# Plain products with whole rows of weights in the first batch's second layer, and its weight sums made a batch later

## The chip, the cores and the metric

The kernel runs on one core of a Trainium2 chip. The metric is the device time of one execution in microseconds (us). Each version was run several times, always beside the kernel before on the same chip; medians are quoted. A profile is one execution out of these, and its "span" is about 1.8 us shorter than the time of the same execution.

Engines in the profile: PE is TensorE (PEld its weight loads), DVE is VectorE, ACT is ScalarE, POOL is GpSimd, SP issues the DMAs. `L1085` is a line of the kernel; L550 is the helper through which all of VectorE's two-input operations go, so these are told apart by their tiles (`s<-h`, `w<-w`).

## The reference

Four batches of 768 x 512. After an attention, each batch goes through a Fourier mix, a normalisation and a channel MLP in float32:

```python
# x: the attention's output, (4, 768, 512)
X = np.fft.fft(np.fft.fft(x, axis=1), axis=2)
u = x + np.real(X).astype(np.float32)
mu = np.mean(u, axis=-1, keepdims=True)
var = np.mean((u - mu) ** 2, axis=-1, keepdims=True)
un = (u - mu) / np.sqrt(var + 1e-06)
ch = np.maximum(un @ w_ch1, 0.0) @ w_ch2      # (512, 2048), then (2048, 512)
return (u + ch).astype(np.float32)
```

The weights come as float64.

## The kernel before

Both layers of the MLP ("h" and "o") multiply in 2x2 blocks with seven block products in place of eight, at the price of sums of blocks: left sums of the first operand, right sums of the second. A batch's MLP goes in two chunks of four hidden tiles (NC = 4): h of chunk 0, o of chunk 0, h of chunk 1, o of chunk 1. In the first batch the weights are converted from float64 piece by piece on VectorE and ScalarE, while the products run; the finished tiles, four blocks and sums in seven slots, are stored to scratch memory, and the later batches only load them.

```python
def _right_sums(tt, b):
    tt(b(T1), b(B12), b(B11), ALU.subtract)
    tt(b(T2), b(B22), b(T1), ALU.subtract)
    tt(b(T3), b(B22), b(B12), ALU.subtract)
    tt(b(T4), b(B21), b(T2), ALU.subtract)
...
    def tt(out, in0, in1, op):                      # L550, VectorE
        nc.vector.tensor_tensor(out=out, in0=in0, in1=in1, op=op)
    def gtt(out, in0, in1, op):                     # L553, GpSimd
        nc.gpsimd.tensor_tensor(out=out, in0=in0, in1=in1, op=op)
...
    def block_sums(b, gg):                          # for the attention of batch b
        ...
        if b == 1:
            tt(raw[0], raw[0], raw[1], ADD)
            nc.vector.tensor_reduce(out=vb, in_=raw[0].rearrange("p f d -> p d f"), op=ADD, axis=AX.X)
        else:
            gtt(raw[0], raw[0], raw[1], ADD)
            while hf > 2:
                hf //= 2
                gtt(raw[0][:, 0:hf], raw[0][:, 0:hf], raw[0][:, hf:2 * hf], ADD)
            gtt(vb, raw[0][:, 0], raw[0][:, 1], ADD)
...
    def make(f, j):                                 # first batch: weight tile j of layer f
        ...
        for hh in range(2):
            yield from convert((f, j, hh), wv[:, 2 * hh:2 * hh + 2].rearrange("p a n -> p (a n)"))
        (_left_sums if f == 1 else _right_sums)(tt, lambda i: wv[:, i])
        yield
        stores.append((to, wv))
        ...
    def get_w2(b, j):
        w = bpool.tile([P, 7, HD], FP, tag="w2", bufs=NC, name=f"w2_{b}_{j}")
        if b == 0:
            return
        fetch(out=w, in_=dw2[j])
        wt[2, b, j] = w
...
    def gen_channel(b):
        ...                                         # h of the chunk, L1038
            for i in range(HT):                     # o: three pairs of row tiles
                ...
                tt(left[S1], a21, left[A22], ADD)   # left sums s<-h
                tt(left[S2_], left[S1], left[A11], SUB)
                tt(left[S3], left[A11], a21, SUB)
                tt(left[S4], left[A12], left[S2_], SUB)
                ...
                def product(ps, a, r, start, stop): # L1085
                    for n, j in enumerate(js):
                        nc.tensor.matmul(ps, left[a][:, n, :], wt[2, b, j][:, r, :], start=start and n == 0,
                                         stop=stop and n == NC - 1, skip_group_check=True)
                product(X, A11, B11, True, False)
                tt(x11, X, x11, ADD)
                ...                                 # six more products, each with its addition
```

Of the kernel before, what the change touches and what calls it, by code (L numbers as in the profile page):

```python
# [16 lines left out]
P = 128  # L17
# [447 lines left out]
def _left_sums(tt, a):  # L465
    tt(a(S1), a(A21), a(A22), ALU.add)
    tt(a(S3), a(A11), a(A21), ALU.subtract)
    tt(a(S2_), a(S1), a(A11), ALU.subtract)
    tt(a(S4), a(A12), a(S2_), ALU.subtract)
# [9 lines that stand above are left out]
def _main_program(ctx, tc, q, k, v, moe_w_ch1, moe_w_ch2, out):  # L479


    nc = tc.nc
    B, H, S, D = q.shape
    DM = H * D
    DF = moe_w_ch1.shape[1]
    NST = S // P
# [11 lines left out]
    NJ = NIT // 2  # L498
    NC = 4
    D1 = D + 1  # L500
    assert (S, DM, D, H % 4, NDT, NJ % NC, WK) == (768, 512, 64, 0, 4, 0, 96)
    ADD, SUB = ALU.add, ALU.subtract
# [30 lines left out]
    dw2 = [dpool.tile([P, 7, HD], FP, name=f"dw2_{j}") for j in range(NJ)]  # L533
# [3 lines left out]
    def fetch(out, in_):  # L537

        ins = nc.sync.dma_start(out=out, in_=in_)
        if in_order[0]:  # L540
            tc.keep_in_program_order(ins)
# [4 lines left out]
    def bank(shape, name):  # L546
        return psum.tile(shape, FP, tag="bank", bufs=4, name=name)

    def tt(out, in0, in1, op):
        nc.vector.tensor_tensor(out=out, in0=in0, in1=in1, op=op)  # L550
# [248 lines left out]
    wt, issued = {}, set()  # L799
# [45 lines left out]
    def make(f, j):  # L845


        if f == 1:
            w = bpool.tile([P, 7, 2, P], FP, tag="w1", bufs=3, name=f"w1_0_{j}")
            wv, to = w.rearrange("p a k n -> p a (k n)"), dw1[j].rearrange("p a k n -> p a (k n)")  # L850
        else:
            w = wv = bpool.tile([P, 7, HD], FP, tag="w2", bufs=NC, name=f"w2_0_{j}")
            to = dw2[j]
        for hh in range(2):
            yield from convert((f, j, hh), wv[:, 2 * hh:2 * hh + 2].rearrange("p a n -> p (a n)"))
        (_left_sums if f == 1 else _right_sums)(tt, lambda i: wv[:, i])
        yield
        stores.append((to, wv))
        if len(stores) > 2 or len(pieces) == len(raws):
            fetch(out=stores[0][0], in_=stores.pop(0)[1])  # L860
        wt[f, 0, j] = w
        yield

    def gen_weights():
        for f, j, stage in plan:
            while stage and stage not in issued:
                yield
            steps = make(f, j)
            while True:

                with tc.issue_after(marks[stage]) if stage in marks else ExitStack():
                    done = next(steps, steps) is steps
                if done:
                    break
                yield
        for to, wv in stores:
            fetch(out=to, in_=wv)

    def get_w1(b, j):
        w = bpool.tile([P, 7, 2, P], FP, tag="w1", bufs=3, name=f"w1_{b}_{j}")  # L880
        if b == 0:
            return
        fetch(out=w, in_=dw1[j])
        wt[1, b, j] = w

    def get_w2(b, j):
        w = bpool.tile([P, 7, HD], FP, tag="w2", bufs=NC, name=f"w2_{b}_{j}")
        if b == 0:
            return
        fetch(out=w, in_=dw2[j])  # L890
        wt[2, b, j] = w


    tables = {}
# [127 lines left out]
    def gen_channel(b):  # L1022
        x, u = x_of[b], wt["u", b]
        for c in range(NJ // NC):
            js = range(NC * c, NC * (c + 1))
            h = bpool.tile([P, NC, 2, S], FP, tag="h", name=f"h_{b}_{c}")
            for j in js:
                if 0 < j < NJ - 2:
                    get_w1(b, j + 2)
                get_w2(b, j)  # L1030
                w = wt[1, b, j]
                c11, c12 = h[:, j - NC * c, 0, 0:S2], h[:, j - NC * c, 0, S2:S]
                c21, c22 = h[:, j - NC * c, 1, 0:S2], h[:, j - NC * c, 1, S2:S]
                X, Y, Z = (bank([P, S2], f"h{n}_{b}_{j}") for n in "xyz")

                def product(ps, a, r, start, stop):
                    for kk in range(2):
                        nc.tensor.matmul(ps, w[:, a, kk, :], u[:, r, kk, :], start=start and kk == 0,  # L1038
                                         stop=stop and kk == 1, skip_group_check=True)

                def relu(t):
                    if b:
                        nc.vector.tensor_scalar(out=t, in0=t, scalar1=0.0, scalar2=None, op0=ALU.max)
                    else:
                        nc.scalar.activation(out=t, in_=t, func=AF.Relu)

                product(X, A11, B11, True, False)
                nc.scalar.copy(out=c11, in_=X)  # L1048
                product(Y, A12, B21, True, True)
                tt(c11, Y, c11, ADD)  # L1050
                yield
                product(X, S2_, T2, False, False)
                nc.scalar.copy(out=c12, in_=X)
                product(Z, S1, T1, True, False)
                nc.scalar.copy(out=c22, in_=Z)
                relu(c11)
                yield
                product(X, S3, T3, False, False)
                tt(c22, X, c22, ADD)
                product(Z, S4, B22, False, True)  # L1060
                tt(c12, Z, c12, ADD)
                yield
                product(X, A22, T4, False, True)
                nc.scalar.activation(out=c21, in_=X, func=AF.Relu)  # L1064
                relu(c22)
                relu(c12)
                issued.add(("h", b, j))
                yield
            for i in range(HT):
                t1, t2 = slice(P * i, P * (i + 1)), slice(S2 + P * i, S2 + P * (i + 1))  # L1070
                left = {A11: h[:, :, 0, t1], A12: h[:, :, 1, t1], A22: h[:, :, 1, t2]}
                for s in (S1, S2_, S3, S4):
                    left[s] = bpool.tile([P, NC, P], FP, tag="s", bufs=5, name=f"s{s}_{b}_{c}_{i}")
                a21 = h[:, :, 0, t2]
                tt(left[S1], a21, left[A22], ADD)
# [3 lines that stand above are left out]
                X, Y, Z = (bank([P, HD], f"o{n}_{b}_{c}_{i}") for n in "xyz")  # L1079
                x11, x12 = x[:, i, 0:HD], x[:, i, HD:DM]  # L1080
                x21, x22 = x[:, HT + i, 0:HD], x[:, HT + i, HD:DM]
# [8 lines that stand above are left out]
                product(Y, A12, B21, True, True)  # L1090
                tt(x11, Y, x11, ADD)
                yield
                product(X, S2_, T2, False, False)
                tt(x12, X, x12, ADD)
                product(Z, S1, T1, True, False)
                tt(x22, Z, x22, ADD)
                yield
                product(X, S3, T3, False, False)
                tt(x22, X, x22, ADD)
                product(Z, S4, B22, False, True)  # L1100
                tt(x12, Z, x12, ADD)
                yield
                product(X, A22, T4, False, True)
                tt(x21, X, x21, ADD)
                if NC * (c + 1) == NJ:
                    for t in (i, HT + i):
                        fetch(out=out[b, P * t:P * (t + 1), :], in_=x[:, t, :])
                if i == HT - 1:
                    issued.add(("o", b, c))
                yield  # L1110

    def gen_post(b):
        yield from gen_fourier(b)
        yield from gen_channel(b)
# [52 lines left out]
    for b in range(B):  # L1167
# [7 lines left out]
        if b == B - 2:  # L1175
# [9 lines left out]
            ps = bank([1, 1], "flag_ps")  # L1185
# [42 lines left out]
```

## Time and profile before

| | before |
|---|---|
| time, median of 3 (range) | 880.09 us (879.41 to 880.5) |
| profiled execution | 881.38 us, span 879.6 us, mean PE clock 0.972 |
| busy: PE, DVE, ACT, POOL | 94%, 57%, 26%, 4% of the span |
| first batch's h and o | 106 to 298.94 us |
| second, third, fourth batch, from the first Fourier product y | at 298.94, 498.78 and 697.53 us |

A batch begins, for the purposes of this text, with its first Fourier product y, which follows the last product of the batch before. The first batch's h and o take 192.7 us, and the whole second batch, with its Fourier mix and the attention that runs beside it, 199.8. So the first batch is where time lies idle. Two rows of GpSimd's timeline before (start, duration, engine, line, operation, tiles, shapes, count, idle before and who ended it), and then two rows of VectorE's:

```profile
263.04 2.37 POOL L553 TENSOR_TENSOR vb<-vb,vb 96x1024 f32<-96x1024 f32 x1 [42.54 <-DMA vb<-in_v_dram]
...
268.98 2.66 POOL L553 TENSOR_TENSOR vb<-vb,vb 96x1024 f32<-96x1024 f32 x1
```

```profile
263.78 2.18 DVE L550 TENSOR_TENSOR s<-s,h 128x512 f32<-128x512 f32 x1
...
269.69 2.50 DVE L550 TENSOR_TENSOR s<-h,s 128x512 f32<-128x512 f32 x1
```

Such a left sum takes 0.68 us elsewhere. PE's waits of 2.46 us at 269.82 and 2.03 us at 278.12, which the prediction shows, end on VectorE's additions right behind these sums.

### The profile page before, as it was taken

How to read it: one execution, taken by the hardware profiler on the slowest of the kernel's cores; microseconds unless marked ns; L12 is line 12 of the kernel's file. 1: busy time of each engine (PE TensorE's matmuls, PEld its weight loads, DVE VectorE, ACT ScalarE, POOL GpSimd, SP SyncE). 2: the span in 40 equal slices, each digit the busy share in tenths (PEclk: the TensorE clock that was granted, in tenths of full speed). 3: DMA queues.
4: the chain of work that ended last, by engine and by line, in shares of the span. 5: the costliest groups of instructions: out<-in, count | busy, mean ns of one | idle time of the engine just before them, and what ended most of it. 6: DMA issues, size and time to landing. Idle time of an engine off the chain costs nothing. (4 is left out here: it accounts for less than half of the span.)

```text
span 879.6 us, 14637 instructions
## 1 busy us (share of the span) xinstructions
PE 826.9 (94%) x6114; PEld 611.7 (70%) x6114; DVE 505.4 (57%) x1111; ACT 229.6 (26%) x473; POOL 36.6 (4%) x38
## 2 busy tenths in 40 slices
PE   5979997889897998999999998999999979999997
PEld 4847654578566875578758875578758866687586
DVE  3588996899999256353339257353329264442252
ACT  3524755521630125412110134410120122101200
POOL 2200002002004000000000000000000000000000
PEclk8969999799999999999999999999999999999999
DMA  9989685976780484341721383220511351305001
GB/s 211 222 225 195 164 210 191 273 257 157 264 296 29 170 223 101 119 116 37 216 84 60 130 242 79 85 86 0 210 55 60 118 224 42 126 1 204 6 26 51
DMA packets 99915, 122.33 MB, mean 139 GB/s; under 512 B 50208, under 2 KB 83200, under 8 KB 99840
## 3 DMA queue, kind: packets, MB, share of 16 engines
q1 hardware_dynamic: 99296, 121.14, 47.4%
q8 instruction: 50, 0.82, 0.4%
q10 hardware_dynamic: 544, 0.17, 0.1%
q14 instruction: 25, 0.20, 0.1%
HBM read 100.32 MB, written 20.97 MB: 138 GB/s over the span
## 5 line engine op out<-in xcount | busy, mean ns | idle before, releaser
L1038 PE MATMUL hx<-u,w 128*128 128x384 f32 x512 | 187.7, 496 | 8.1 <-ACT h L1048 5.3
L1038 PEld LDWEIGHTS hx<-u,w 128*128 128x128 f32 x512 | 95.8, 192 | 76.0 <-ACT h L1048 7.3
L1085 PE MATMUL ox<-w,s 128*128 128x256 f32 x384 | 91.9, 382 | 3.6 <-DVE x L550 3.6
L1038 PE MATMUL hz<-u,w 128*128 128x384 f32 x256 | 94.3, 487 | 0.0
L1085 PE MATMUL ox<-w,h 128*128 128x256 f32 x384 | 91.3, 386 | 2.5 <-DVE x L550 2.5
L1085 PE MATMUL oz<-w,s 128*128 128x256 f32 x384 | 91.8, 379 | 0.4 <-DVE s L550 0.4
L1085 PEld LDWEIGHTS ox<-w,h 128*128 128x128 f32 x384 | 73.7, 193 | 14.6 <-DVE x L550 2.9
L1085 PEld LDWEIGHTS ox<-w,s 128*128 128x128 f32 x384 | 71.8, 190 | 15.5 <-DVE x L550 5.6
L1085 PEld LDWEIGHTS oz<-w,s 128*128 128x128 f32 x384 | 72.9, 190 | 10.4 <-DVE s L550 0.5
L550 DVE TENSOR_TENSOR x<-ox,x 128x256 f32<-128x256 f32 x96 | 40.3, 422 | 67.7 <-PE ox L1085 67.5
L1038 PEld LDWEIGHTS hz<-u,w 128*128 128x128 f32 x256 | 48.8, 191 | 34.1 <-issue 0.6
L550 DVE TENSOR_TENSOR h<-hy,h 128x384 f32<-128x384 f32 x32 | 17.8, 556 | 61.0 <-PE hy L1038 60.9
L960 ACT COPY big<-y 128x192 f32<-128x192 f32 x32 | 10.6, 337 | 150.3 <-PE y L954 150.2
L1038 PE MATMUL hy<-u,w 128*128 128x384 f32 x128 | 46.5, 486 | 0.0
L1085 PE MATMUL oy<-w,h 128*128 128x256 f32 x192 | 46.4, 382 | 0.0
L550 DVE TENSOR_TENSOR h<-hx,h 128x384 f32<-128x384 f32 x32 | 17.8, 556 | 48.3 <-PE hx L1038 48.3
L1048 ACT COPY h<-hx 128x384 f32<-128x384 f32 x32 | 15.3, 477 | 102.8 <-PE hx L1038 98.6
L655 DVE TENSOR_REDUCE km<-kt 128x24 f32<-128x768 f32 x16 | 15.2, 951 | 45.6 <-ACT kt L654 32.8
L1085 PEld LDWEIGHTS oy<-w,h 128*128 128x128 f32 x192 | 36.7, 192 | 5.8 <-DVE w L550 0.4
L1064 ACT ACTIVATE h<-hx 128x384 f32<-128x384 f32 x32 | 15.7, 490 | 85.9 <-PE hx L1038 85.8
L550 DVE TENSOR_TENSOR x<-oz,x 128x256 f32<-128x256 f32 x48 | 20.3, 423 | 30.9 <-PE oz L1085 30.9
L954 PE MATMUL y<-fs,fold 128*128 128x193 f32 x192 | 36.4, 333 | 0.0
(117 smaller groups left out, 1117.2 us busy)
## 6 DMA issues: line engine op xcount, KB each, us to landing
w<-dw SPq DMA_DIRECT2D x48, 896.0 KB, 5.6
raw<-in_moe_w_ch_dram SPq DMA_DIRECT2D x32, 512.0 KB, 5.6
dw<-w SPq DMA_DIRECT2D x16, 896.0 KB, 6.7
vw<-in_v_dram SPq DMA_DIRECT2D x47, 192.0 KB, 5.3
kn<-in_k_dram SPq DMA_DIRECT2D x16, 384.0 KB, 5.4
qn<-in_q_dram SPq DMA_DIRECT2D x16, 384.0 KB, 5.7
vb<-in_v_dram SPq DMA_DIRECT2D x16, 384.0 KB, 7.2
out_dram<-x SPq DMA_DIRECT2D x24, 256.0 KB, 2.0
```

What stands on the lines that cost most here:

```text
L550: nc.vector.tensor_tensor(out=out, in0=in0, in1=in1, op=op)
L655: nc.vector.tensor_reduce(out=km[:, 0:nb], in_=kt[:, W:W + S].rearrange("p (n f) -> p n f", f=BLOCK), op=ALU.max, axis=AX.X)
L954: nc.tensor.matmul(y, fgs[par][:, st, P * g:P * (g + 1)], fs[par][:, g % 2, st, :], start=(st == 0), stop=(st == HT - 1))
L960: nc.scalar.copy(out=ty[:, g, par:S2:2], in_=y[:, 0:F2])
L1038: nc.tensor.matmul(ps, w[:, a, kk, :], u[:, r, kk, :], start=start and kk == 0, stop=stop and kk == 1, skip_group_check=True)
L1048: nc.scalar.copy(out=c11, in_=X)
L1064: nc.scalar.activation(out=c21, in_=X, func=AF.Relu)
L1085: nc.tensor.matmul(ps, left[a][:, n, :], wt[2, b, j][:, r, :], start=start and n == 0, stop=stop and n == NC - 1, skip_group_check=True)
```

## The change

In the first batch VectorE is full with the conversion of weights. The change takes the sums of the second layer out of that batch: its second layer becomes a plain matrix product, with whole rows of 512 weights at a time, which needs neither left sums of h nor right sums of w2. The tiles are stored with their four plain blocks. The second batch loads those, makes the right sums on VectorE, uses them and stores the seven slots for the third and fourth batch. The price is more work for PE.

```diff
@@ make
-        (_left_sums if f == 1 else _right_sums)(tt, lambda i: wv[:, i])
+        if f == 1:
+            _left_sums(tt, lambda i: wv[:, i])
+        else:
+            to, wv = to[:, 0:4], wv[:, 0:4]
@@ get_w2
-        fetch(out=w, in_=dw2[j])
         wt[2, b, j] = w
+        if b == 1:
+            fetch(out=w[:, 0:4], in_=dw2[j][:, 0:4])
+            _right_sums(tt, lambda i: w[:, i])
+            fetch(out=dw2[j][:, 1:7], in_=w[:, 1:7])
+        else:
+            fetch(out=w, in_=dw2[j])
@@ gen_channel
+            if b == 0:
+                for t in range(NST):
+                    ps = bank([P, DM], f"o_{b}_{c}_{t}")
+                    for n, j in enumerate(js):
+                        for hf in range(2):
+                            nc.tensor.matmul(ps, h[:, n, hf, P * t:P * (t + 1)], wt[2, b, j][:, 2 * hf:2 * hf + 2, :],
+                                             start=(n, hf) == (0, 0), stop=(n, hf) == (NC - 1, 1))
+                        if n % 2 == 0:
+                            yield
+                    tt(x[:, t, :], ps, x[:, t, :], ADD)
+                    if NC * (c + 1) == NJ:
+                        fetch(out=out[b, P * t:P * (t + 1), :], in_=x[:, t, :])
+                issued.add(("o", b, c))
+                continue
```

## The prediction

> **What bounds the kernel now.** I read the overview's slices first, then the groups by line and form, then the stages as windows, then the timelines of TensorE (PE) and VectorE (DVE) over the first batch's channel part, since the change touches mainly that.
>
> ```profile
> PE   5979997889897998999999998999999979999997
> DVE  3588996899999256353339257353329264442252
> ```
>
> A slice is 22 us. The first batch's channel part (first layer h, second layer o, two chunks each) runs from 106 to 299 us, slices 5 to 13; the other batches follow. From slice 14 on PE is full nearly always and DVE mostly half idle: PE is the bound. In slices 5 to 12 DVE is at 9, as it converts the 32 weight pieces there. The same as windows (columns: busy us and instructions of PE, weight loads, DVE, ACT, POOL; granted PE clock; DMA share; GB/s), with h and o of chunk 0, a mixed stretch between them, then h and o of chunk 1:
>
> ```profile
> 106.00:158.00 52.00, 46.15 (x377) 26.40 (x379) 42.85 (x83) 31.19 (x61) 5.81 (x5) 0.97 0.68 199
> 158.00:179.00 21.00, 16.74 (x221) 10.85 (x210) 17.38 (x38) 11.25 (x21) 0.00 (x0) 0.76 1.09 282
> 179.00:217.00 38.00, 36.47 (x276) 31.10 (x274) 36.44 (x81) 8.62 (x14) 2.70 (x2) 1.00 0.69 185
> 217.00:256.00 39.00, 36.78 (x115) 21.09 (x114) 36.79 (x79) 22.38 (x43) 3.27 (x4) 1.00 0.82 284
> 256.00:299.00 43.00, 38.52 (x170) 32.89 (x169) 32.52 (x54) 0.49 (x1) 11.73 (x8) 0.96 0.27 83
> ```
>
> The middle three show PE and DVE both almost full. In 158 to 179 PE's figure flatters: the clock was 0.76. PE's timeline shows where it stands (start, us, group, idle before and who ended it):
>
> ```profile
> 138.32 2.93 PE L1038 MATMUL hx<-u,w 128*128 128x384 f32 x4 [3.35 <-ACT h L1048]
> ...
> 172.39 2.77 PE L1038 MATMUL hx<-u,w 128*128 128x384 f32 x4
> ...
> 178.57 1.99 PE L1085 MATMUL oz<-w,s 128*128 128x256 f32 x8 [0.35 <-DVE s L550]
> ...
> 224.60 1.56 PE L1038 MATMUL hx<-u,w 128*128 128x384 f32 x4 [2.18 <-ACT h L1053]
> ...
> 269.82 4.25 PE L1085 MATMUL ox<-w,h 128*128 128x256 f32 x12 [2.46 <-DVE x L550]
> ...
> 278.12 1.99 PE L1085 MATMUL ox<-w,s 128*128 128x256 f32 x8 [2.03 <-DVE x L550]
> ```
>
> The bracketed waits of PE from 106 to 299 add up to 18.3 us. Adding matmuls run at a reduced clock after such pauses, my ledger of lost PE time is: about 2.5 us in small waits; 5 at 134-141; 10.5 in 158-178.6 (20.5 us elapsed; the matmuls there cost some 10 us at the rates below); 2 in 182-198; 2.2 at 224; 6.5 in 266-279. That is 29 us, some 25 of it due to DVE. The large 10.5 is DVE's queue: from 153 to 169 it works through three second-layer weight tiles without a pause, and only then gets to the evictions that finish h of the fourth hidden tile:
>
> ```profile
> 167.68 1.09 DVE L550 TENSOR_TENSOR w<-w 128x256 f32<-128x256 f32 x3
> 168.69 0.42 DVE L833 TENSOR_SCALAR cvt<-raw 128x512 int32<-128x512 int32 x1
> 169.03 0.55 DVE L550 TENSOR_TENSOR h<-hx,h 128x384 f32<-128x384 f32 x1
> ```
>
> **What the Trainium skill says.** (1) "TensorE: Matmul & The Clock Gate", Back-to-back issue gap, gives N / 2.4 + 2.5 ns at the warm clock. Here every float32 matmul of the program is recorded twice (1344 records of the o line, 672 calls), and each record takes twice N at that rate: the chain of waits has eight 256-column records in 1.73 us, 216 ns each, and four 384-column ones in 1.29 us, 323 ns. So four column times a call, which agrees with the page "FP8 and Floating Point Precision", TensorE Precision Notes (true FP32 takes four passes). The per-matmul cost is some 3 ns, so that wider matmuls gain almost nothing. (2) "SBUF — State Buffer", two separate sides: VectorE with two SBUF inputs and GpSimd block each other for a whole instruction. The trace agrees: an SBUF-to-SBUF sum of 0.68 us took 2.18 us at 263.78, while GpSimd ran. Sums from PSUM kept 0.42 us. (3) "Perfetto Trace Analysis", Optimizing Scalar/DVE Operations: fewer, larger operations save fixed time. The trace agrees: in the saturated stretches DVE starts 128x256 additions 0.335 us apart and 128x512 ones 0.60 apart, so one wide one saves 0.07 us over two narrow ones.
>
> **The change part by part.**
>
> *PE, first batch.* Seven products of 256 columns per row pair and hidden tile become plain products of 512 columns. Before: 3 row pairs x 7 products x 4 hidden tiles x 2 chunks = 168 calls, 336 records x 216 ns = 72.6 us (batch 3 runs its two chunks in 36.3 us each, which agrees). After: 6 row tiles x 8 half hidden tiles x 2 chunks = 96 calls, 192 records. The line through 216 ns at 256 and 323 at 384 gives 429 ns at 512: 82.4 us. PE has 9.8 us more to do, all of it on the bound engine. Weight loads (190 ns a record) stay hidden under 429 ns.
>
> *DVE, first batch.* Gone: left sums, 24 of 128x512 x 0.60 = 14.4 us; right sums, 8 tiles x 4 x 0.335 = 10.7 us; evictions, 42 x 0.335 = 14.1 us become 12 x 0.60 = 7.2 us. Together 32 us fewer of about 166 us busy.
>
> *DMA, first batch.* Eight stores of 896 KB become 512 KB, 3.1 MB less.
>
> *Second batch.* DVE gets the 10.7 us of right sums; loads become 512 KB, and eight stores of 768 KB are new. DVE was busy 17.0 of 40 us in the window 340 to 380, so there is room, and those stores are needed only a batch later. Batches 3 and 4 are unchanged.
>
> *What the freed DVE time is worth on the path.* Around 158-178: 11 right sums lie ahead of the delayed h evictions, 3.7 us, and the four left sums between h and the first S product, 2.4 us, vanish: some 6.5 us of the 10.5. At 182-198: 1.5 of 2. At 224: about 1.3 of 2.2 (four more tiles lose their sums there). At 266-279: all 6.5, since the left sums that GpSimd stretched are no longer between PE and its next product, and the output additions read PSUM. At 134-141 the wait is ACT behind a conversion that GpSimd stretched; only the earlier right sums come off, 1 us. Sum: 16.8 us saved. Less 9.8 us of PE work: the first batch ends 7 us sooner.
>
> *What the second batch takes back.* Four right sums come in a burst of 1.4 us a tile, ahead of that tile's evictions in program order. First-layer PSUM tiles have roughly one product (1.29 us) of slack against an eviction of 0.56 us, so that a collision costs a few tenths. One or two in each of 8 hidden tiles: 2 us. Net: -5 us, 880 to 875.
>
> **The rivals.**
>
> *A: PE bounds and the extra products are not paid for.* If the stalls of the first batch just move (DVE's queue holds the same conversions, which wait on weight loads when DMA is full, 1.09 in the second window), only the left sums' share is won, 6 to 8 us, and the time is 880 + 9.8 + 2 - 7 = 885. For it: PE already full in the last windows, DMA over 1 in the worst stretch. Against: 17 us of the ledger end on DVE or on ACT behind DVE, and stores shrink.
>
> *B: nearly all stalls vanish.* With DVE a fifth emptier, the conversions run ahead and also 134-141 and the small waits go: 26 of the 29 us saved, 880 - 26 + 9.8 + 1 = 865. Against: 134-141 is GpSimd's lock, which stays.
>
> *C: the second batch stalls.* VectorE's queue is in order; if its right sums are placed ahead of a load that lands later than planned, the evictions behind them wait, and PE with them; or the issuing queue holds a first-layer load back behind the new store. In chunk 1 the tile's buffer comes free only at the end of the previous o, and a load takes 5.6 us to land. With 2 us at each of 8 tiles: 16 us more, 889. Against: first-layer weights are fetched two tiles ahead, 18 us, and the order of the queues is planned with the landing in view.
>
> **Range and chances.** The centre is 875. A and B give 865 to 885; the whole ledger limits the gain, and C seems less likely than a small part of it. Eight times in ten: 866 to 885. Over 2% faster means below 862.5, more than 17.6 us, which needs B to be more than complete: 0.05. Over 2% slower, above 897.7, needs A and C together: 0.02. The rest, 0.93, is within 2%.
>
> **What would show it right or wrong.** Right: the o line of the first batch shows 192 records of 128x512 with starts 0.43 us apart; no left sums before the second batch; the second batch's first Fourier product starts near 292 instead of 298.94 us; no PE wait over 1 us on DVE in its second o; the wait around 135-141 still there; the distance from that Fourier product to the end grows by 1 to 3 us. Wrong: the second batch starting later than 297 (A), before 284 (B), or new waits of PE's first layer on DVE, or of DVE on a weight load, of over 5 us in sum in the second batch (C). Another order of the instructions in the first batch, which this change can cause, is what would most easily upset the sum: the 10.5 us wait comes from such an order, not from a lack of DVE time as such.

## The result, and the profile after

| | before | after |
|---|---|---|
| median, same rounds | 880.3 us, 4 runs | 869.82 us, 4 runs (868.97 to 875.3) |
| ratio, 95% interval | | 0.989 (0.9853 to 0.9928) |
| profiled execution | 881.38 us | 875.3 us, the slowest of the four |
| second, third batch's first y | 298.94, 498.78 us | 291.13, 490.95 us |

The ratio is the mean time of one kernel's runs over that of the other's of the same rounds, so it is not quite the ratio of the medians. By it the change saves 1.1%, within the 2% that count as the same, though the interval is clear of 1. The result is correct.

The overview after, PE and DVE in 40 slices of 22 us:

```profile
PE   5979998998999999999999999999999979999997
DVE  3487995985982384353548165353349164442252
```

In slices 7 to 13 (counted from 1 here; the prediction counts from 0) PE stood at 7 to 9 before and is now at 8 and 9, and DVE, at 9 in slices 9 to 13 before, is at 8, 5, 9, 8 and 2. As windows by stage (busy us and instructions of PE, weight loads, DVE, ACT, POOL; PE clock; DMA share; GB/s):

```profile
106.00:158.00 52.00, 46.96 (x437) 27.42 (x436) 41.22 (x77) 31.41 (x62) 5.65 (x5) 0.97 0.72 209
158.00:179.00 21.00, 21.00 (x152) 10.14 (x152) 20.75 (x46) 10.42 (x18) 0.00 (x0) 1.00 1.07 275
179.00:212.00 33.00, 30.55 (x188) 14.88 (x187) 25.90 (x48) 12.00 (x21) 5.90 (x5) 0.95 0.80 237
212.00:250.00 38.00, 37.09 (x115) 21.35 (x114) 26.60 (x49) 20.17 (x39) 5.11 (x4) 1.00 0.72 238
250.00:291.00 41.00, 41.00 (x97) 18.21 (x96) 19.56 (x31) 0.49 (x1) 6.96 (x4) 1.00 0.22 74
```

From 158 to 179 us, PE was busy 16.74 us at a clock of 0.76 before; now it is busy for all 21.00 at full clock, though VectorE is even fuller there than it was (20.75 us after 17.38). The last stage, 250 to 291, is without a gap. The plain products in the groups by line (busy us and mean ns of one; the matmuls overlap, so that 603 ns is a latency and not the distance between two):

```profile
L1084 PE MATMUL o<-w,h 128*128 128x512 f32 x192 | 85.7, 603 | 0.0
```

192 records, as worked out; the 96 of the second chunk run from 249.93 to 291.13 us, 0.43 us each. PE's timeline after, at the places where the prediction looked for waits:

```profile
136.74 2.76 PE L1047 MATMUL hx<-u,w 128*128 128x384 f32 x4 [2.74 <-ACT h L1057]
...
157.94 1.13 PE L1084 MATMUL o<-w,h 128*128 128x512 f32 x2
158.90 1.46 PE L1047 MATMUL hx<-u,w 128*128 128x384 f32 x4
160.20 6.42 PE L1084 MATMUL o<-w,h 128*128 128x512 f32 x14
...
208.02 1.14 PE L748 MATMUL av<-vs,p 64*128 64x130 f32 x12 [2.45 <-DVE vs L550]
209.09 3.43 PE L1084 MATMUL o<-w,h 128*128 128x512 f32 x4
...
291.13 1.48 PE L963 MATMUL y<-fs,fold 128*128 128x193 f32 x8
```

The last product of the fourth hidden tile now runs at 158.90 us; before it was at 172.39. The reason stands in VectorE's timeline: the eviction `h<-hx,h` that PE needs was at 169.03 us before, behind three weight tiles. Now it is

```profile
158.19 0.55 DVE L550 TENSOR_TENSOR h<-hx,h 128x384 f32<-128x384 f32 x1
```

The wait at 136.74 has stayed, as predicted. One at 208.02 is new, and the four wide products after it take 3.43 us, twice their 1.72: the granted clock was 0.50 from 209.09 to 210.70. The wait ends on a small operation of VectorE's (`vs<-vs,half`, at 207.69), which queued behind the conversion; two of the conversion's multiplications (`w<-cvt`) took 3.42 us together beside GpSimd's block sums, which run from 199.72 us on.

### The profile page after: what moved, and what is told of

It is laid out like the page before. It is cut to its first block, busy times and chain, and to the rows that moved or that the text cites. A ratio compares the mean times of both kernels' runs of the same rounds, so it can differ in the third digit from the quotient of the medians.

```text
span 873.5 us, 14326 instructions
## 1 busy us (share of the span) xinstructions
PE 829.8 (95%) x5970; PEld 582.2 (67%) x5970; DVE 482.5 (55%) x1057; ACT 230.2 (26%) x473; POOL 36.1 (4%) x38
## 5 line engine op out<-in xcount | busy, mean ns | idle before, releaser
L1084 PE MATMUL o<-w,h 128*128 128x512 f32 x192 | 85.7, 603 | 0.0
L1109 PE MATMUL ox<-w,s 128*128 128x256 f32 x288 | 68.8, 382 | 0.0
L1109 PE MATMUL oz<-w,s 128*128 128x256 f32 x288 | 68.4, 380 | 0.0
L1109 PE MATMUL ox<-w,h 128*128 128x256 f32 x288 | 66.4, 379 | 0.0
L1084 PEld LDWEIGHTS o<-w,h 128*128 128x128 f32 x192 | 36.6, 193 | 44.4 <-issue 42.3
L550 DVE TENSOR_TENSOR x<-ox,x 128x256 f32<-128x256 f32 x72 | 30.4, 423 | 61.0 <-PE ox L1109 60.8
L1109 PEld LDWEIGHTS ox<-w,h 128*128 128x128 f32 x288 | 54.8, 190 | 8.6
L1109 PEld LDWEIGHTS ox<-w,s 128*128 128x128 f32 x288 | 54.1, 190 | 8.7 <-DVE x L550 1.4
L1109 PEld LDWEIGHTS oz<-w,s 128*128 128x128 f32 x288 | 54.9, 190 | 7.3
L1047 PEld LDWEIGHTS hy<-u,w 128*128 128x128 f32 x128 | 24.7, 193 | 17.4 <-issue 0.9
```

The costliest lines, as they stand in the source:

```text
L1047: nc.tensor.matmul(ps, w[:, a, kk, :], u[:, r, kk, :], start=start and kk == 0, stop=stop and kk == 1, skip_group_check=True)
L1084: nc.tensor.matmul(ps, h[:, n, hf, P * t:P * (t + 1)], wt[2, b, j][:, 2 * hf:2 * hf + 2, :], start=(n, hf) == (0, 0), stop=(n, hf) == (NC ...
```

## The experiments

Twelve runs, in four groups; every one gave the right result. The times of one group were taken on one chip, with the kernel before beside them: the first four rows of the table below (after_again to plain_early_sums), the next four, the next three, and the last. "y at" is the first Fourier product of the second batch, the end of the first batch, in the profile, which is one execution and not the median. The diffs below are cut to the main lines: where the plain products move, the conditions in `make` and `get_w2` move with them, so that each tile gets its sums in the first batch that needs them.

| kernel | time, us | before, us | ratio (95%) | y at |
|---|---|---|---|---|
| after_again | 870.15 | 879.15 | 0.9891 (0.9863 to 0.9919) | 286.77 |
| plain_chunk0 | 869.85 | 879.15 | 0.9876 (0.9849 to 0.9902) | 289.42 |
| plain_chunk1 | 876.06 | 879.15 | 0.9947 (0.9922 to 0.9972) | 296.32 |
| plain_early_sums | 871.59 | 879.15 | 0.9908 (0.9881 to 0.9934) | 289.14 |
| vector_blocks | 863.8 | 881.4 | 0.9804 (0.9787 to 0.9822) | 280.99 |
| chunk0_vector_blocks | 856.75 | 881.4 | 0.9733 (0.9716 to 0.975) | 274.57 |
| before_vector_blocks | 866.51 | 881.4 | 0.9823 (0.98 to 0.9846) | 285.83 |
| plain_two | 879.49 | 881.4 | 0.9986 (0.9968 to 1.0003) | 287.74 |
| before_first_vector | 876.53 | 880.5 | 0.9966 (0.9949 to 0.9982) | 296.84 |
| idle_left_sums | 869.67 | 880.5 | 0.989 (0.9867 to 0.9912) | 287.36 |
| late_thrice | 868.94 | 880.5 | 0.9871 (0.9853 to 0.9889) | 287.94 |
| idle_all_sums | 873.09 | 880.11 | 0.9927 (0.9904 to 0.995) | 291.81 |

### The change once more, and each half of it

**after_again** is the kernel after, unchanged.

> The changed kernel itself, once more, unchanged. The profile after had a span of 873.5 us while its other runs took 869 to 870.4. My theory: the first product of the second batch starts at 291 us again (298.9 before), and everything behind it shifts by the same 7.8 us through the second batch; the rest of the 10.5 us, and the 6 us by which the profiled run was longer, lie elsewhere and a second profile shows where. Expected 869 to 871 timed. Rival: the 7.8 us itself varies from run to run, and the first product of the second batch starts anywhere between 286 and 291.

It gave 870.15 us (868.91 to 873.68). The times are as the theory had them, but y is not: the profile of this quicker execution has it at 286.77 us, 12.2 us ahead of before rather than 7.8, within the rival's range. The two profiles of one kernel part at the new wait. PE's timeline here:

```profile
206.48 0.94 PE L748 MATMUL av<-vs,p 64*128 64x130 f32 x12 [1.18 <-DVE vs L550]
207.35 1.98 PE L1084 MATMUL o<-w,h 128*128 128x512 f32 x4
...
286.77 1.47 PE L963 MATMUL y<-fs,fold 128*128 128x193 f32 x8
```

The wait is 1.18 us instead of 2.45, and after it the four products run at full clock, 1.98 us instead of 3.43. Wait and clock make some 2.7 us of the 4.4 us between the profiles; a wait of 0.89 us at 245.95, which only the first has, is most of the rest. So one execution's shift is not the kernel's: 7.8 belongs to the slowest of its round. The 12.2 is a little too much, since the profile of before that it is taken from was itself 1.1 us above its median; by the medians the gain is 9.0 us here and 10.5 in the first rounds.

**plain_chunk0** has plain products in chunk 0 only; the weights of chunk 1 keep early sums and seven products.

```diff
-            if b == 0:
+            if b == 0 and c == 0:
```

> Plain products in the first batch's chunk 0 only; chunk 1 keeps the seven products, left sums and early right sums as before. By the ledger of the prediction chunk 0 alone wins 6.5 + 1.5 + 1 us and pays 4.9, so 4 us of gain; chunk 1 wins 7.8 and pays 4.9, so 3 us. Theory (both chunks pay): 872 to 876, between before and after. Rival (with the wait of chunk 0 gone, VectorE is ahead, and the seven products of chunk 1 would no longer stall): 866 or less, faster than after.

**plain_chunk1** is the reverse.

```diff
-            if b == 0:
+            if b == 0 and c == 1:
```

> The other half alone: plain products in chunk 1 only. Theory (both chunks pay): 874 to 878, and the 10 us stretch of lost TensorE time around 160 to 178 us is there again as before. Rival (the gain is all in chunk 0): 880 or more, the products of chunk 1 costing 4.9 us for nothing.

The halves gave 9.3 and 3.1 us, both together 9.0. In plain_chunk1 the stall at 158 to 177 us is there as before, and the theory's range held. In plain_chunk0 that stall is gone, and although seven products in chunk 1 spare PE half of the 9.8 us, one long wait takes it back. PE's timeline of plain_chunk0:

```profile
256.12 3.67 PE L1110 MATMUL ox<-w,s 128*128 128x256 f32 x8 [5.54 <-DVE x L550]
```

and VectorE's just before it, while GpSimd works from 245.36 to 259 us:

```profile
245.73 2.53 DVE L550 TENSOR_TENSOR s<-h 128x512 f32<-128x512 f32 x1 [0.59 <-ACT h L1055]
...
252.91 2.82 DVE L550 TENSOR_TENSOR s<-h,s 128x512 f32<-128x512 f32 x1
255.66 0.41 DVE L550 TENSOR_TENSOR x<-ox,x 128x256 f32<-128x256 f32 x1
```

The left sums of chunk 1, about four times their usual length, hold the addition that PE's next product waits for. Neither expectation hit: the chunk is as fast as the whole change. What the second half of the change does is to get out of GpSimd's way.

### Is it VectorE's amount of work, or what stands before what?

**plain_early_sums** puts three of the four right sums of each w2 tile back into the first batch, where nothing needs them (the fourth would overwrite a plain block). The plain products stay.

```diff
         else:
-            to, wv = to[:, 0:4], wv[:, 0:4]
+            tt(w[:, T1], w[:, B12], w[:, B11], SUB)
+            tt(w[:, T2], w[:, B22], w[:, T1], SUB)
+            tt(w[:, T4], w[:, B21], w[:, T2], SUB)
```

> As the changed kernel, but three of the four right sums of each second-layer tile stay in the first batch (8 us of VectorE there, and stores of 896 KB again); only the fourth, which overwrites an operand of the plain products, is made in the second batch. Theory (VectorE time in the first batch is on the path): 3 to 6 us slower than after, 873 to 876. Rival (the left sums and the shorter way from h to the second layer made the gain, and the right sums were hidden): within 1 us of after.

**idle_left_sums** puts back the 24 left sums, made on VectorE and never read.

```diff
             if b == 0:
+                for i in range(HT):
+                    ...
+                    tt(s1, h[:, :, 0, t2], h[:, :, 1, t2], ADD)
+                    tt(s2, s1, h[:, :, 0, t1], SUB)
+                    tt(s3, h[:, :, 0, t1], h[:, :, 0, t2], SUB)
+                    tt(s4, h[:, :, 1, t1], s2, SUB)
```

> The kernel after, with the left block sums of the first batch's hidden tiles (four sums of 128x512 for each of three row pairs and two chunks, 24 in all) made on VectorE as in the kernel before, ahead of the plain products, and never read. The result stays right. Theory (the gain of the plain products comes from the waits of TensorE on those sums and on what they hold up, and VectorE has some 40 us of spare time between 106 and 290 us): PE doesn't wait for them, except where evictions queue behind them, so the time rises by at most 3 us, to 870 to 873 us (ratio 0.988 to 0.992). Rival (the gain is VectorE's capacity: its 24 sums of some 0.7 us, 17 us, and longer beside GpSimd, are on the path): the time rises by 5 to 12 us, to 875 to 882 us, and the kernel is no faster than before.

**idle_all_sums** has both edits.

> The kernel after with nearly all of VectorE's old work put back into the first batch and none of it used there: the 24 left block sums of the hidden tiles are made and never read (as in idle_left_sums, which cost nothing), and three of the four right sums of each of the second layer's weight tiles are made early (as in plain_early_sums, 1.5 us slower than after). The plain products stay. Theory (order and dependence: the change gains because no product of the first batch's second layer waits for a sum, not because VectorE has less to do): the time is that of plain_early_sums, 870 to 873 us (ratio to before 0.988 to 0.992), with the stall after 158 us still small. Rival (amount: either part alone fits into VectorE's spare time, both together do not): the conversion of the last weight tiles comes later, a wait of some 4 to 8 us opens between 158 and 180 us, and the time is 875 to 880 us.

The right sums cost 1.4 us against after_again, less than the theory then expected and more than the rival; the two intervals overlap, so even that is not clear of noise. The left sums cost nothing: 869.67 us. Both together: 873.09 us, 7.0 us below before. That is 0.1 above the range of order and dependence and outside that of amount, though the interval (871.7 to 875.7 us) touches both. VectorE's busy time in the same window of three kernels, before, after_again and idle_all_sums (columns as above):

```profile
106.00:290.00 184.00, 165.65 (x1094) 114.41 (x1095) 163.86 (x326) 73.92 (x140) 23.52 (x18) 0.95 0.69 206
```

```profile
106.00:290.00 184.00, 177.76 (x999) 93.12 (x997) 132.62 (x254) 75.02 (x142) 24.84 (x18) 0.99 0.68 203
```

```profile
106.00:290.00 184.00, 174.41 (x974) 90.30 (x973) 156.33 (x292) 74.67 (x139) 24.55 (x18) 0.98 0.70 213
```

The change took 31 us of work off VectorE; idle_all_sums has 24 of them again and keeps two thirds of the gain. Nor has the 158 us stall come back, though VectorE is busy there for 21.00 us of the 21 from 158 to 179, where it was 17.38 before; PE is at 20.59. Its timeline in idle_all_sums:

```profile
157.01 0.42 DVE L550 TENSOR_TENSOR w<-w 128x256 f32<-128x256 f32 x1
157.35 0.69 DVE L839 SCALAR_TENSOR_TENSOR cvt<-raw,cvt 128x512 f32<-128x512 uint32 x1
157.95 0.55 DVE L550 TENSOR_TENSOR h<-hx,h 128x384 f32<-128x384 f32 x1
158.42 0.68 DVE L550 TENSOR_TENSOR w<-cvt 128x512 f32<-128x512 f32 x1
159.01 0.42 DVE L832 TENSOR_SCALAR cvt<-raw 128x512 int32<-128x512 int32 x1
159.35 0.42 DVE L550 TENSOR_TENSOR w<-w 128x256 f32<-128x256 f32 x1
```

and PE's:

```profile
158.56 1.56 PE L1048 MATMUL hx<-u,w 128*128 128x384 f32 x4
159.95 5.31 PE L1092 MATMUL o<-w,h 128*128 128x512 f32 x12
165.67 3.67 PE L1092 MATMUL o<-w,h 128*128 128x512 f32 x8 [0.41 <-DVE w L550]
```

The weight sums `w<-w` are back in the queue, but the eviction stands between them at 157.95 us instead of behind all of them. What the work put back does cost stands elsewhere, at the wait near 208 us beside GpSimd:

```profile
208.52 1.67 PE L748 MATMUL av<-vs,p 64*128 64x130 f32 x12 [3.65 <-DVE vs L550]
210.12 3.78 PE L1092 MATMUL o<-w,h 128*128 128x512 f32 x4
```

So most of the gain is not amount but order (evictions ahead of the conversion) or dependence (no product of this layer needs a sum). Some 3 us may be amount; the same wait differs by nearly as much between two executions of the kernel after (2.45 and 1.18 us, with and without half the clock). Which of order and dependence it is, no run separates: sums that nothing reads can be laid out anywhere, and some 7 of the 31 us (the fourth right sum and what the wider evictions save) were not put back.

**before_first_vector** tried to get that order without the plain products: the kernel before, with block sums on VectorE (as in before_vector_blocks below) and the MLP given precedence when the instructions are laid out.

```diff
-        if b == 1:
+        if b >= 1:
...
-            drive((gen_channel(0), 4, 0), (weights, 12, 0), (attn, 1, 0))
+            drive((gen_channel(0), 4, 600), (weights, 12, 0), (attn, 1, 0))
```

> The kernel before, with the block sums of the third and fourth batches on VectorE (as in before_vector_blocks) and with the first batch's channel stage given first place in the order of emission, so that the evictions and right block sums of the fourth hidden tile stand ahead of the sums of the last pieces of the second layer's weights in VectorE's queue. No product and no sum is added or taken away against before_vector_blocks. Theory (the long stall after 158 us is one of order on VectorE, not of its amount of work; the change closed it because the weights' sums were what stood in front): the stall after the first chunk's hidden tiles shrinks from about 10 us to under 4 us, y of the second batch starts 5 to 8 us sooner than in before_vector_blocks, and the time is 857 to 862 us (ratio to the kernel before 0.972 to 0.979), without a single plain product. Rival (it is the amount: VectorE has no spare time in that stretch, so that whatever is put back comes due in another wait before the first chunk's last product): the stall moves by under 2 us, to wherever the weights' sums now stand, and the time stays at 864 to 868 us.

Both expectations missed: 876.53 us, 10 us worse than before_vector_blocks. The products of h of the fourth tile did run through (the last before 158.4 us), but PE stood 3.63 us at 142.97, ahead of an attention product and with no releaser shown, and what then came due was the weights' own sums, in PE's timeline:

```profile
170.49 1.13 PE L1085 MATMUL ox<-w,h 128*128 128x256 f32 x4 [2.13 <-DVE w L550]
...
174.64 1.22 PE L1085 MATMUL oy<-w,h 128*128 128x256 f32 x2 [2.19 <-DVE w L550]
...
177.78 2.08 PE L1085 MATMUL ox<-w,h 128*128 128x256 f32 x4 [1.93 <-DVE w L550]
```

and the attention of the second batch, pushed back, was left over at the end: from 288.81 us on PE has only that for 8 us, until y at 296.84. The edit moves the attention as well as the evictions, so it doesn't separate the two; it shows that precedence for the MLP is not what the change does.

### What the second batch pays

**late_thrice** makes the right sums of the second batch again and again, with the same values in the end: 64 sums more.

```diff
             _right_sums(tt, lambda i: w[:, i])
+            for _ in range(2):
+                tt(w[:, T1], w[:, B12], w[:, B11], SUB)
+                tt(w[:, T2], w[:, B22], w[:, T1], SUB)
+                for _ in range(2):
+                    tt(w[:, T4], w[:, B21], w[:, T2], SUB)
```

> The kernel after, with the right weight sums of the second batch made again: two more times the first, second and fourth sum, and the fourth four more times in all, which leaves the same values. Each of the eight hidden tiles then costs VectorE eight sums more, 64 in all by about 0.7 us, some 43 us of work added in the second batch. Theory (the sums cost nothing there, since VectorE has far more idle time in that batch than they take and they are made well ahead of their use): the time from y of the second batch to y of the third stays within 1 us of 199.8 us, and the total within 1 us of the kernel after (869 to 872 us). Rival (they are hidden only because they are few; VectorE's queue holds evictions behind them): the second batch takes 3 us or more longer, and the total is 873 to 878 us.

It gave 868.94 us, and the theory held. But the expectation took a sum at 0.7 us; one of these is only 128x256, and they added 21 us to VectorE in the second batch, a third of a microsecond each, rather than 43 us. The windows of after_again and of late_thrice:

```profile
290.00:490.00 200.00, 196.71 (x1602) 146.45 (x1600) 104.88 (x247) 45.03 (x98) 0.63 (x2) 1.00 0.44 132
```

```profile
290.00:490.00 200.00, 196.41 (x1596) 146.31 (x1595) 125.94 (x313) 45.17 (x98) 0.64 (x2) 1.00 0.45 132
```

PE is as full with 125.94 us of VectorE's work as with 104.88. From y to y the second batch takes 200.23 us against 199.85 in after_again. The 32 sums that the change moved there cost nothing that can be seen.

**plain_two** gives the second batch plain products too; the third makes the sums.

```diff
-            if b == 0:
+            if b < 2:
```

> Plain products in the second batch as well; the right sums move on to the third. This is the price of the plain products by themselves, in a batch where VectorE is half idle. Theory (TensorE is the bound there, nothing is won): 9.8 us slower than after, 878 to 881. Rival (shorter ways between the engines win something there too): less than 5 us slower.

879.49 us, as the theory had it. The third batch's y is at

```profile
497.22 1.48 PE L965 MATMUL y<-fs,fold 128*128 128x193 f32 x8
```

which is 209.5 us after the second's (287.74), where the other kernels need 199.8. The plain products cost 9.6 us where PE is the bound; the first batch's stalls paid for them, the second batch has none.

### GpSimd's part

The waits that the change left (136.74, 208.02) and the one of plain_chunk0 stand beside GpSimd's block sums, so these were put on VectorE for the third and fourth batch too, as they already are for the second: first in the kernel after, then with plain products in chunk 0 alone, then in the kernel before. The edit is one line:

```diff
-        if b == 1:
+        if b >= 1:
```

**vector_blocks**: the kernel after, with it.

> The changed kernel, but the value block sums of batches 3 and 4, which GpSimd made inside the first batch, are made by VectorE (as those of batch 2 are). GpSimd then runs nothing from 100 us on. Theory (the waits left in the first batch, around 136, 206 and 245 us, come from GpSimd blocking VectorE's two-input sums): the long 128x512 sums of 2.4 and 2.8 us are back to 0.7, most of those waits are gone, and the time falls by 3 to 6 us to 864 to 867, although VectorE gets about 12 us more to do. Rival (VectorE's amount of work is the bound there): 2 to 6 us slower than after.

**chunk0_vector_blocks**: plain_chunk0, with it.

> Plain products in chunk 0 only, and the block sums on VectorE. The run with plain products in chunk 0 alone was as fast as the changed kernel although TensorE had 4.9 us less to do, because its second o stood 5.5 us behind left sums that took up to 2.8 us beside GpSimd. Theory: without GpSimd that wait is below 1 us and the time is 862 to 865, the fastest so far. Rival (the left sums together with the fold of the second batch are too much for VectorE in any case): within 1 us of the run with plain products in chunk 0 alone.

**before_vector_blocks**: the kernel before, with it.

> The kernel before, with the block sums on VectorE: how much of what the change won could be had without it. Theory (the long wait at 158 to 178 is a matter of VectorE's queue and stays; only the waits at 136, 224 and 266 to 279 are GpSimd's): 873 to 877. Rival 1 (GpSimd was the whole trouble): 870 or less. Rival 2 (VectorE was simply full): 881 or more.

The one line in the kernel before saves 14.9 us, more than the change that this text is about, though it gives VectorE more to do. The theory (873 to 877) missed and the first rival's range (870 or less) held, but not its reason, that GpSimd was the whole trouble. The prediction's ledger has 5, 2.2 and 6.5 us for the stalls at 134 to 141, 224 and 266 to 279; these go, but for 0.4 us, and y moves by 13.1. The left sums of chunk 1 there, in VectorE's timeline, with nothing on GpSimd:

```profile
257.38 0.68 DVE L550 TENSOR_TENSOR s<-s,h 128x512 f32<-128x512 f32 x1
...
259.93 0.68 DVE L550 TENSOR_TENSOR s<-h,s 128x512 f32<-128x512 f32 x1
```

0.68 us where they took 2.18 and 2.50. What stays is the stall of chunk 0. All of it lies 4.8 us earlier, but the eviction stands behind the same three weight tiles, and from the first `ox` product to the first `oz` PE takes 19.9 us as before (154.00 to 173.86, where it was 158.74 to 178.57).

```profile
164.27 0.55 DVE L550 TENSOR_TENSOR h<-hx,h 128x384 f32<-128x384 f32 x1
```

With all of the change the line saves 17.6 us in all, 0.2 beyond the range of the theory, and with the first half of the change 24.7, where 862 to 865 us had been expected. So the savings of chunk 0's plain products (9.3) and of the block sums (14.9) add up, as they close different stalls. The second half of the change closed the same stalls as the block sums on VectorE do, and then only its 4.9 us of extra PE work is left. The windows of chunk0_vector_blocks:

```profile
106.00:180.00 74.00, 71.40 (x596) 38.46 (x595) 64.48 (x134) 40.73 (x76) 0.00 (x0) 1.00 0.85 246
180.00:275.00 95.00, 94.94 (x453) 64.03 (x452) 77.49 (x159) 31.61 (x59) 0.00 (x0) 1.00 0.61 188
```

PE is full at full clock from 106 us to the end of the first batch, but for 2.7 us. (Of its lead of 7.1 us over vector_blocks, 1.8 us arose before the first product of h in the profiles, with no cause shown; the rest is about the 4.9 us of PE work. The 24.7 above holds these 1.8 us too.) At 856.75 us, ratio 0.9733, it is the fastest version.

## Why the prediction was right, and where it was off

It said 875 us and, most likely, within 2%; it came to 869.8, at 0.989.

Two of its readings were loose: VectorE is not at 9 in all of slices 5 to 12 (6 and 8 stand among them), and the ledger's share that is due to VectorE is 25 us in one place and 17 in another; the bracketed waits of the first batch that end on VectorE come to 7.5 us and those on ScalarE's copies of h to 7.8.

**PE's 9.8 us** were right. 192 records, 0.43 us apart; plain_two pays 9.6 us for the same thing where PE bounds.

**VectorE's 32 us** were right as an amount (163.86 to 132.62 us in the same window, in after_again). The prediction took the amount for the means, at least in part; idle_all_sums shows that giving 24 us back costs at most some 3 us of time.

**The stall at 158 to 178.6** is the first mis-sized term: "some 6.5 us of the 10.5" by counting the sums ahead of the delayed evictions and those before the first S product. All 10.5 vanished: PE is busy for 21.00 us of 21.00. The eviction didn't come 3.7 us sooner, with fewer sums ahead of it, but 10.8 us sooner, ahead of the rest of the conversion. The last sentence of the prediction names this ("from such an order, not from a lack of DVE time as such") but its sum does not use it. Why the layout of instructions puts the eviction first once the products are plain is not shown by any run; that it is tied to chunk 0's plain products is (plain_chunk0 and plain_chunk1), and that it is not tied to the sums' being gone is too (idle_all_sums, where six of every seven sums are back).

**The other stalls** of the first batch: at 266 to 279 all 6.5 us went, as predicted. At 134 to 141 the wait on ACT stayed, as predicted (2.74 us after 3.35). The small waits at 182 to 198 and the 2.18 at 224 went, but a new wait at 208 came, 2.45 us and half a clock in one profile and 1.18 us in the other, and one of 0.89 at 245.95 in the first. On the prediction's own ledger 11.4 of 29 us of PE time are still lost in the first profile, so 17.6 were saved where it said 16.8, and less 9.8 that makes the 7.8 us by which y moved (7 were predicted). That agreement is partly chance: the undervalued stall and the new wait cancel in that profile, and in after_again's y moves by 12.2.

**The second batch's 2 us** is the second mis-sized term: 0. The shift of y, 7.81 us at the second batch, is 7.83 at the third; late_thrice adds twice as many sums again without a trace of it in the time. So collisions of the sums with evictions, each of "a few tenths", do not happen on the path. One sign came true by luck: the stretch from y to the end was to grow by 1 to 3 us, and in the first profile it is 1.7 us longer (582.4 after 580.7); but these arise after the fourth batch's y, where nothing was changed, and in after_again it is 580.7 again.

**Rivals.** A (stalls only move, 885) fell with the end of chunk 0's stall; a little of it is true, in the wait at 208. B (nearly all vanish, 865) was held off by just what spoke against it, GpSimd's lock (sums of VectorE's stretched while GpSimd works); with the lock taken away, vector_blocks came to 863.8. C (the second batch stalls) did not occur at all.

So of the 5 us between the predicted and the measured time, 2 are the second batch and the rest the stall of chunk 0, valued too low, less what the new wait took, which differs from one execution to the next. The prediction also saw GpSimd's lock in the trace and used it only as a bound on the gain; by before_vector_blocks it was the larger prize.

## What to carry to other kernels

When a stall is put down to a full engine, put the removed work back where nothing reads it: if the time hardly moves, as here, the stall was one of order or dependence, and its worth is its whole length, not the length of the work removed. (Which of the two, this test does not say.) More arithmetic pays only in the stage where the bound engine was standing still: the same plain products won some 10 us in the first batch and lost 9.6 in the second. And before routing work around a slow stretch, ask what makes it slow: moving GpSimd's few sums to the engine that looked overfull won more than the change, and half of the change was only a detour around them.

## What the Trainium skill lacked or had wrong

- "TensorE: Matmul & The Clock Gate", What's actually happening and Back-to-back issue gap: the clock is said to fall after an idle window of about 3.4 us. Here it also fell after shorter waits of PE. After 2.45 us four 512-column records took 3.43 us, at a granted clock of 0.50 at first; in the kernel before, after 2.46 us at 269.82, right behind dense products, twelve 256-column records took 4.25 us, at 0.50 from 272 to 274. After waits of 1.18 us (1.98 us for the same four) and, in the kernel before, of 2.03 us (eight 256-column records in 1.99 us) the clock was 1.00, while after 2.04 us in plain_early_sums four 512-column records took 3.56 us. So a wait need not reach 3.4 us to cost half the clock, and its length alone does not decide. The sustained figure there for N = 512, about 131 ns, is not what float32 sees: 430 ns a record, two records a matmul; the page has no float32 row.
- "SBUF — State Buffer", two separate sides: the rule of the lock agrees with the lines shown, but the page does not say how much a chain of short sums loses. Here sums of 0.68 us took 2.18 to 2.82 us beside GpSimd sums of some 2.4 us, and 14.9 us of an 881 us kernel hung on 18 GpSimd instructions that are busy for 24 us.
